# Window attention and two feed-forward layers on one core: means of v from pairs added by GpSimd, unread products in the first microseconds, the first h ahead of the transposes, all keys loaded ahead of v

## The chip, the core and the metric

One core of a Trainium2 chip runs the whole program. It has five engines, each with its own queue of instructions in program order: TensorE (PE in the profile) multiplies matrices into PSUM, VectorE (DVE), ScalarE (ACT) and GpSimd (POOL) work elementwise, and SyncE (SP) here issues every DMA. An engine that waits for a semaphore holds up everything behind it in its own queue. The metric is the device time of one execution in microseconds (us), the median of the runs; less is better.

## What is computed

The output is a chain of three: attention in a window with block summaries, then two feed-forward layers. Cut to what matters:

```python
# q, k, v: 2 batches, 8 heads, 768 positions, 64 wide
k_sum = k.reshape(B, H, nb, 32, D).max(axis=3)     # block maxima of the keys
v_sum = v.reshape(B, H, nb, 32, D).mean(axis=3)    # block means of v
scores_l = scale * q @ k.T, masked to |i - j| < 16
scores_s = scale * q @ k_sum.T + log(32)
a = softmax(concat(scores_l, scores_s))
x = a @ concat(v, v_sum)                           # 1536 tokens, 512 wide

h = x @ w_in                                       # 512 -> 2048
g = max(h, 0) + alpha * min(h, 0)
x = g @ w_out                                      # 2048 -> 512

h = x @ w_in2; g = P(h) / (Q(h) + 1e-6)            # rational function
out = g @ w_out2
```

## The kernel before

The feed-forward products run on operands that are split into a high and a low part, each of which PE multiplies in fp32r: three products (high x high, high x low, low x high) make one. `h_mm` makes h for 128 of the 2048 inner columns in twelve products, `y_mm` adds these 128 inner columns to y in twelve. Weights come as 1 MB transfers (`raw`), and a sequence of steps takes each apart: `top` on ScalarE, `cv` on VectorE ("low"), the high part on ScalarE ("hi": wih, woh), and the two halves of the low part on GpSimd ("mid", "end": wil, wol).

Attention goes by tiles of 64 queries, 24 of them (n). One tile passes through: `qk` (scores s on PE, for four pairs of heads), `mask` and `max` on VectorE, `exp` on ScalarE, `sum`, `guard` and `inv` for the divisor, `norm` (p times 1/d, on GpSimd or VectorE), `turn` (PE transposes p into PSUM, pt), `turned` (ScalarE copies it to pT), `pv` (PE: po), `out` and `outl` (po split into the high and low x, xh on ScalarE and xl on VectorE). PSUM holds one tile each of s, pt and po.

A first loop runs over steps t = -1 to 27. In each step the list of `ORDERS` for the phase of t is gone through, word by word, and each word issues the work of one stage, for n = t plus an offset (qk of t, exp of t - 1, turn of t - 2, pv of t - 3). This fixed order is the order on each engine: nothing is moved at run time. `ENG` says which engine a copy or small step has in each of six phases. "H" and "Y" issue h and y of the first feed-forward layer in the gaps of attention: H from t = 6, Y from t = 9. After the loop the rest of the h and y runs alone, to the end at about 616 us.

The block means of v need all positions of a batch. `att_vload` loads 128 positions of v (`vt`, four buffers), `att_vmean` multiplies them by a matrix `mean` that has 1/32 in the right places, and adds up six such products in one bank of PSUM (`vps`). `VMEAN_AT` gives the step t of each of the twelve. After the sixth, ScalarE copies the means to SBUF, and GpSimd puts them under the values (`vc`) that pv multiplies. `att_kmax` takes the block maxima of the keys (`kmax` from `kt`), which stand beside the keys of each tile in `kc`. `FIRST` lists the first transfers: k0 and k1 are the two halves of the first batch's keys in four transfers each, v tiles, and q tiles. `keep_busy` multiplies the identity with itself into a bank of PSUM that is not read (`idle`).

Of the kernel before, what the change touches and what calls it, by code (L numbers as in the profile page):

```python
# [9 lines left out]
F32 = mybir.dt.float32  # L10
# [21 lines left out]
N_FIRST = 3  # L32
EARLY = 8

VMEAN_AT = (-1, -1, 0, 0, 1, 2, 6, 7, 8, 9, 9, 9)
VLOAD_T = 4
KMAX_AT = (6, 6, 6, 7, 9, 9, 9, 10)
KLOAD_AT = (4, 7)
# [5 lines left out]
     "guard v act in act H gh new"),  # L44
    ("act qk sum hi mid turn act vm k act mask in exp v vmean gh gl max pv ks guard out inv sub low turned "
     "end Y outl kmax H new norm"),
    ("qk vm k exp hi act mask max pv sum out Y turn sub mid inv gl guard in low outl act v vmean act norm H "
     "turned new ks end kmax gh"),
    ("gh qk act pv ks act act exp out end mask hi k sum gl max vmean outl low kmax turn guard mid Y v vm in "
     "sub inv turned new H norm"),  # L50
# [3 lines left out]
     "low guard ks Y end H norm"),  # L54
)

FIRST = 'k0 v0 v1 k1 q0 q2 v2 v3 q1'

SOFTMAX = 'aaaassasaasssabssssssass'

ENG = {"guard": "vapppv", "k": "vpaaaa", "turned": "aaaaaa", "vm": "apppaa", "ks": "ppppav", "norm": "vppppp", "sub": "pppppp",
       "gl": "vvvppp", "gh": "vapaaa", "hi": "vaaaaa", "mid": "pvpppp", "end": "pppppp", "out": "aaaaaa", "al": "vavaaa"}

LEAD = (4, 6, 4, 4, 9, 13, 5, 10)
# [1 line left out]
CLOSE_E = 10  # L66
NKC = 2
VM_WITH = {0: (0, 1), 1: (2, 3)}
BUSY = {(3, 'pv'): 6, (4, 'pv'): 4, (5, 'qk'): 4, (6, 'qk'): 2}


@with_exitstack
def kernel(
# [228 lines left out]

    ident = a1.tile([P, P], F32, name="ident")
    make_identity(nc, ident)
    NQZ, NVC, NVT = 3, 4, 4
    vlate = []
    HALF = S // 2 + 2 * WINDOW
    HSUB = NSUB // 2
    NV = S // P
    bias = []  # L310
    for e in range(3):
        t = a1.tile([P, KEYS], F32, name=f"bias{e}")
# [13 lines left out]
    qz = [b1.tile([P, NPAIR, 2 * QS], F32, name=f"qz{i}") for i in range(NQZ)]  # L326
    kc = [b1.tile([P, NPAIR, KEYS], F32, name=f"kc{i}") for i in range(NKC)]
    vc = [a1.tile([KEYS, DM], F32, name=f"vc{i}") for i in range(NVC)]
    mean = e1.tile([P, KEYS + NB - P // BLOCK], F32, name="mean")
    nc.gpsimd.memset(mean, 0.0)  # L330
    for i in range(P // BLOCK):
        c0 = KEYS - P // BLOCK + i
        nc.gpsimd.memset(mean[i * BLOCK:(i + 1) * BLOCK, c0:c0 + 1], 1.0 / BLOCK)
    kt, kmax, vt, vmean, st = {}, {}, {}, {}, {}

    def att_load(b, half):
# [12 lines left out]
            axis=AX.X, op=ALU.max)  # L349

    def att_vload(b, i):
        vt[b, i] = e1.tile([P, DM], F32, tag="vt", name="vt", bufs=NVT)
        s0 = WINDOW + i * P
        nc.sync.dma_start(out=vt[b, i], in_=vS[b, s0:s0 + P, :])

    def att_vmean(b, i):

        if i == 0:
            vmean[b] = psy.tile([P, 512], F32, tag=f"y{b}", name="vps")
        z0 = (NV - 1 - i) * (P // BLOCK)  # L360
        nc.tensor.matmul(out=vmean[b][0:KEYS, :], lhsT=mean[:, z0:z0 + KEYS], rhs=vt[b, i],  # L361
                         start=(i == 0), stop=(i == NV - 1))
        n = b * NV + i + NVT
        if n < B * NV:
            vlate.append(n)
        if i == NV - 1:
            ps, vmean[b] = vmean[b], (b1 if b else e1).tile([KEYS, DM], F32, tag=f"vmean{b}", name=f"vmean{b}")
            nc.scalar.copy(vmean[b][STRIP:KEYS, :], ps[STRIP:KEYS, :])
# [215 lines left out]
    with tc.manual_schedule():  # L584
        for step in FIRST.split():
            {"k": lambda i: att_load(0, i), "v": lambda i: att_vload(0, i), "q": att_in}[step[0]](int(step[1]))
        for i in range(2 * NPAIR):
            att_kmax(0, i)
        for i, at in enumerate(VMEAN_AT):
            if at == -2:  # L590
                att_vmean(*divmod(i, NV))
        for t in range(-1, LAST + 1):
            now[0] = t
            if t == CLOSE_E:
                att_e.close()
                w_place(1)
            if t == NQ:
                att_qk.close()
                w_place(2)
            if t == 4:  # L600
                nc.sync.dma_start(out=al, in_=alpha)
            if t == 8:
                nc.sync.dma_start(out=na, in_=pa.partition_broadcast(P))
                nc.sync.dma_start(out=ab, in_=pb.partition_broadcast(P))
            if t == 12:
                nc.scalar.mul(na, na, -1.0)
                nc.scalar.activation(out=ab, in_=ab, func=AF.Abs)
            if t in KLOAD_AT:
                att_load(1, KLOAD_AT.index(t))
            act = acts.pop(0) if acts else iter(())  # L610
            g = later.pop(t, None)
            for step in ORDERS[sum(t >= at for at in PHASES)].split():
                if step in attn:
                    f, o = attn[step]
                    for n in {t + o, t + o - (o < -1)}:
                        if 0 <= n < NQ and n - t - o == -(o < -1 and n >= EARLY):
                            f(n)
                    keep_busy(t, step)
                elif step in every:
                    every[step](t)  # L620
                elif step == "act":
                    next(act, None)
                elif step in ("gh", "gl"):
                    if g:
                        (g_split if step == "gh" else g_low)(*g)
                else:
                    w_step(step, 2 if step == "new" else 0)
            if t in WLOAD_AT:
                w_load(*loads.pop(0))
        for act in acts:  # L630
            for _ in act:
                pass
        for t in sorted(later):
            g_split(*later[t])
            g_low(*later[t])
# [104 lines left out]
```

## Time and profile before

| what | value |
|---|---|
| median of 3 runs | 617.39 us (616.64 to 617.71) |
| the profiled execution | 617.73 us |
| its span, first to last instruction | 615.9 us |
| PE busy | 597.7 us (97%), 3224 products |
| VectorE, ScalarE, GpSimd busy | 338.7, 379.9, 358.4 us |
| DMA | 55.09 MB, 89 GB/s on average, over 300 GB/s in most of the first 46 us |
| chain that ended last | PE 76%, VectorE 11%, ScalarE 6%, DMA 3% |

The span begins with the first instruction and is 1.8 us shorter than the time of its execution. A product in fp32 (all of attention) shows in the profile as two rows, one in fp32r as one. The shares are averages over a first stage, in which all engines and the DMA take turns, and a long second one. The granted clock of PE is given as a share of full speed.

### The profile page before, as it was taken

To read this page: it belongs to the slowest core of one execution; us is meant where nothing else is said; L and a number is where in the kernel's file an instruction comes from. 1 tells how busy PE (TensorE), PEld (TensorE's weight loads), DVE (VectorE), ACT (ScalarE), POOL (GpSimd) and SP (SyncE) were. 2 spreads that over 40 slices of the span, in tenths; PEclk is the share of its full clock that TensorE was granted. 3 is DMA by queue.
4 is the path that set the end of the run, shared out by engine and by line. 5 is a ranking of instruction groups with operands and counts; after the bars stand their busy time and mean duration, and the time that the engine had idled before them with its cause. 6 is when DMAs were issued, how large, how long until landed. Compare 5 with 4: busy or idle time off the path is not lost.

```text
span 615.9 us, 8657 instructions
## 1 busy us (share of the span) xinstructions
PE 597.7 (97%) x3224; PEld 498.4 (81%) x3224; DVE 338.7 (55%) x494; ACT 379.9 (62%) x659; POOL 358.4 (58%) x349
## 2 busy tenths in 40 slices
PE   5989999999999999999999999999999999999996
PEld 2767989988888888888888888888888888888884
DVE  4767687753221111145555277776566666566664
ACT  1768898877443333367777467776566666566663
POOL 3467789666612222237777558776466666466662
PEclk9989999999999999999999999999999999999999
DMA  8997566525100000024555101000100000100001
GB/s 299 323 349 248 199 211 220 194 81 206 68 1 1 1 0 1 0 87 187 205 180 185 48 0 69 0 2 1 68 2 1 0 1 1 69 0 2 2 0 68
DMA packets 17129, 55.09 MB, mean 89 GB/s; under 512 B 2368, under 2 KB 4416, under 8 KB 12992
## 3 DMA queue, kind: packets, MB, share of 16 engines
q1 hardware_dynamic: 17088, 54.55, 25.2%
q8 instruction: 25, 0.41, 0.3%
q14 instruction: 16, 0.13, 0.1%
HBM read 51.39 MB, written 3.15 MB: 89 GB/s over the span
## 4 chain that ended last, share of the span: by engine, by line
PE 76%; DVE 11%; ACT 6%; DMA 3%; POOL 2%; issue 1%; SPq 1%; DVEq 0%; ACTq 0%
PE h L197 35%; PE y L260 35%; DVE tp L232 2%; PE s L403 2%; DVE tp L222 2%; DVE h L231 2%; DVE tu L230 2%; DMA kt<-in_kT 2%; ACT h L228 2%; ACT h L229 2%; DVE tp L221 1%; PE vps L361 1%; PE pt L459 1%; PE po L473 1%; DMA qz<-in_qT 1%
## 5 line engine op out<-in xcount | busy, mean ns | idle before, releaser
L197 PE MATMUL h<-xh,wih 128*128 128x512 f32 (+1 forms) x416 | 156.4, 376 | 0.5 <-DVE tp L210 0.5
L197 PE MATMUL h<-xl,wih 128*128 128x512 f32 (+1 forms) x416 | 155.4, 374 | 0.0
L197 PE MATMUL h<-xh,wil 128*128 128x512 f32 (+1 forms) x416 | 155.2, 373 | 0.0
L244 POOL TENSOR_TENSOR gl<-tp,gh 128x512 fp32r<-128x512 f32 (+1 forms) x75 | 95.2, 1270 | 80.1 <-ACT gh L139 78.6
L139 ACT ACTIVATE gh<-tp 128x512 fp32r<-128x512 f32 (+1 forms) x76 | 46.2, 608 | 91.5 <-DVE tp L232 44.6
L197 PEld LDWEIGHTS h<-xh,wih 128*128 128x128 f32 x416 | 78.7, 189 | 15.0 <-DVE tp L210 0.7
L197 PEld LDWEIGHTS h<-xl,wih 128*128 128x128 f32 x416 | 78.6, 189 | 14.0 <-issue 0.5
L197 PEld LDWEIGHTS h<-xh,wil 128*128 128x128 f32 x416 | 78.6, 189 | 13.8
L260 PE MATMUL y<-gh,woh 128*128 128x512 f32 (+1 forms) x224 | 81.9, 366 | 0.0
L260 PE MATMUL y<-gh,wol 128*128 128x512 f32 (+1 forms) x224 | 80.4, 359 | 0.0
L260 PE MATMUL y<-gl,woh 128*128 128x512 f32 (+1 forms) x224 | 80.3, 359 | 0.0
L260 PE MATMUL y<-woh,gh 128*128 128x512 f32 x192 | 74.8, 390 | 1.1 <-ACT gh L139 1.1
L165 DVE SCALAR_TENSOR_TENSOR cv<-raw,top 128x1024 int32<-128x1024 int32 x32 | 58.8, 1838 | 30.4 <-ACT top L163 23.9
L260 PE MATMUL y<-wol,gh 128*128 128x512 f32 x192 | 74.7, 389 | 0.0
L260 PE MATMUL y<-woh,gl 128*128 128x512 f32 x192 | 74.5, 389 | 0.0
L230 DVE SCALAR_TENSOR_TENSOR tu<-tu,h 128x512 f32<-128x512 f32 x48 | 33.0, 687 | 71.0 <-ACT h L229 67.5
L219 POOL TENSOR_SCALAR tu<-tv,ab 128x512 f32<-128x512 f32 x48 | 37.2, 776 | 57.9 <-ACT tv L217 57.9
L220 POOL TENSOR_TENSOR tu<-tu,tv 128x512 f32<-128x512 f32 x48 | 62.3, 1298 | 4.0
L244 POOL TENSOR_TENSOR gl<-tu,gh 128x512 fp32r<-128x512 f32 (+1 forms) x28 | 33.2, 1184 | 49.0 <-ACT gh L139 48.9
L210 DVE SCALAR_TENSOR_TENSOR tp<-h,tp 128x512 f32<-128x512 f32 (+1 forms) x28 | 17.2, 614 | 69.0 <-ACT tp L139 69.0
L228 ACT ACTIVATE h<-tu,lnb 128x512 f32<-128x512 f32 x48 | 33.2, 692 | 35.1 <-DVE tp L222 32.7
L210 DVE SCALAR_TENSOR_TENSOR tu<-h,tu 128x512 f32<-128x512 f32 (+1 forms) x28 | 17.2, 613 | 62.0 <-ACT tu L139 62.0
(83 smaller groups left out, 1066.9 us busy)
## 6 DMA issues: line engine op xcount, KB each, us to landing
raw<-in_w_in SPq DMA_DIRECT2D x16, 1024.0 KB, 4.6
raw<-in_w_out SPq DMA_DIRECT2D x16, 1024.0 KB, 4.6
qz<-in_qT SPq DMA_DIRECT2D x25, 256.0 KB, 5.2
vc<-in_vS SPq DMA_DIRECT2D x24, 192.0 KB, 5.2
kt<-in_kT SPq DMA_DIRECT2D x16, 208.0 KB, 5.0
vt<-in_vS SPq DMA_DIRECT2D x12, 256.0 KB, 5.1
out<-stage SPq DMA_DIRECT2D x12, 256.0 KB, 2.1
al<-in_alpha SPq DMA_DIRECT2D x1, 8.0 KB, 5.5
```

The costliest lines, as they stand in the source:

```text
L139: e.activation(out=out, in_=in_, func=AF.Copy, scale=1.0 if scale is None else scale)
L165: nc.vector.scalar_tensor_tensor(out=w.bitcast(I32), in0=rest, scalar=13, in1=top, op0=ALU.logical_shift_right, op1=ALU.bitwise_or)
L197: nc.tensor.matmul(out=ps, lhsT=a, rhs=b, start=(c == 0 and m == 0), stop=(c == NC - 1 and m == 2))
L210: nc.vector.scalar_tensor_tensor(out=t, in0=ps, scalar=0.0, in1=t, op0=ALU.max, op1=ALU.subtract)
L219: nc.gpsimd.tensor_scalar(out=q, in0=v, scalar1=ab[:, 1:2], scalar2=ab[:, 0:1], op0=ALU.mult, op1=ALU.add)
L220: nc.gpsimd.tensor_tensor(out=q, in0=q, in1=v, op=ALU.mult)
L222: nc.vector.scalar_tensor_tensor(out=p, in0=p, scalar=na[:, 1:2], in1=ps, op0=ALU.add, op1=ALU.mult)
L228: nc.scalar.activation(out=A, in_=q, func=AF.Ln, scale=2.0 ** -LN_SHIFT, bias=lnb)
L229: nc.scalar.activation(out=A, in_=A, func=AF.Exp, scale=-1.0, bias=exb)
L230: nc.vector.scalar_tensor_tensor(out=q, in0=q, scalar=one, in1=A, op0=ALU.add, op1=ALU.mult)
L244: (eng("gl") if (u, f) != steps[-1] else nc.vector).tensor_tensor(out=gl, in0=t, in1=gh.bitcast(F32), op=ALU.subtract)
L260: nc.tensor.matmul(out=yps[c][:, c0:c0 + n] if layer == 0 else yps[c], lhsT=a, rhs=b, start=(f == 0 and c0 == 0 and m == 0), stop=(f == NF ...
```

## The change

Four things. A tile of v now holds 256 positions, two consecutive ones in each partition; GpSimd adds the two, and PE multiplies the sum, so that there are three products for a batch instead of six, and two buffers instead of four. `mean` is built with 16 partitions to a block. `FIRST` loads both halves of the keys, then q0 and q1, and only then v. Eighteen products of the identity stand first on PE, and more of them at t = 6 (three behind qk, three behind pv). In the list of t = 5 and 6, pv and out come earlier, H comes ahead of turn and vmean, outl ahead of the "low" step, and guard moves from GpSimd to VectorE, ahead of inv.

```diff
-VMEAN_AT = (-1, -1, 0, 0, 1, 2, 6, 7, 8, 9, 9, 9)
+VMEAN_AT = (0, 1, 2, 6, 7, 9)
...
-    ("qk vm k exp hi act mask max pv sum out Y turn sub mid inv gl guard in low outl act v vmean act norm H "
-     "turned new ks end kmax gh"),
+    ("qk pv vm k exp out hi act mask max sum guard inv outl H Y turn sub mid norm gl in low act v vmean act "
+     "turned new ks end kmax gh"),
...
-FIRST = 'k0 v0 v1 k1 q0 q2 v2 v3 q1'
+FIRST = 'k0 k1 q0 q1 v0 q2 v1'
...
-ENG = {"guard": "vapppv", "k": "vpaaaa", "turned": "aaaaaa", "vm": "apppaa", "ks": "ppppav", "norm": "vppppp", "sub": "pppppp",
+ENG = {"guard": "vavppv", "k": "vpaaaa", "turned": "aaaaaa", "vm": "apppaa", "ks": "ppppav", "norm": "vppppp", "sub": "pppppp",
...
-BUSY = {(3, 'pv'): 6, (4, 'pv'): 4, (5, 'qk'): 4, (6, 'qk'): 2}
+BUSY = {(-2, ''): 18, (3, 'pv'): 6, (4, 'pv'): 4, (5, 'qk'): 4, (6, 'qk'): 3, (6, 'pv'): 3}
...
-    NQZ, NVC, NVT = 3, 4, 4
+    NQZ, NVC, NVT = 3, 4, 2
...
-    NV = S // P
+    NV = S // (2 * P)
...
-        vt[b, i] = e1.tile([P, DM], F32, tag="vt", name="vt", bufs=NVT)
-        s0 = WINDOW + i * P
-        nc.sync.dma_start(out=vt[b, i], in_=vS[b, s0:s0 + P, :])
+        vt[b, i] = e1.tile([P, 2, DM], F32, tag="vt", name="vt", bufs=NVT)
+        s0 = WINDOW + i * 2 * P
+        nc.sync.dma_start(out=vt[b, i], in_=vS[b, s0:s0 + 2 * P, :].rearrange("(p a) c -> p a c", a=2))
...
-        z0 = (NV - 1 - i) * (P // BLOCK)
-        nc.tensor.matmul(out=vmean[b][0:KEYS, :], lhsT=mean[:, z0:z0 + KEYS], rhs=vt[b, i],
+        z0 = (NV - 1 - i) * VB
+        v = vt[b, i]
+        nc.gpsimd.tensor_tensor(out=v[:, 0, :], in0=v[:, 0, :], in1=v[:, 1, :], op=ALU.add)
+        nc.tensor.matmul(out=vmean[b][0:KEYS, :], lhsT=mean[:, z0:z0 + KEYS], rhs=v[:, 0, :],
                          start=(i == 0), stop=(i == NV - 1))
...
+        keep_busy(-2, "")
         for i in range(2 * NPAIR):
             att_kmax(0, i)
```

At t = 5 and 6 the order on PE stands as follows, first before the change, from the scores of t = 5 to the first product of h.

```order
L403 MATMUL s<-kc_182,qz_180 128x120 x4
L494 MATMUL idle<-ident 128x128 x4
L473 MATMUL po<-pT,vc_185 64x64 x8
L459 MATMUL pt<-ident,p 120x128 x4
L403 MATMUL s<-kc_181,qz_178 128x120 x4
L494 MATMUL idle<-ident 128x128 x2
L473 MATMUL po<-pT,vc_186 64x64 x8
L459 MATMUL pt<-ident,p 120x128 x4
L361 MATMUL vps<-vt,mean 120x512
L197 MATMUL h<-xh,wih_432 128x256
```

After the change, on PE from the scores of t = 6 to those of t = 7, of the twelve products of h the first and the last:

```order
L410 MATMUL s<-kc_181,qz_178 128x120 x4
L501 MATMUL idle<-ident 128x128 x3
L480 MATMUL po<-pT,vc_186 64x64 x8
L501 MATMUL idle<-ident 128x128 x3
L197 MATMUL h<-xh,wih_450 128x256
...
L197 MATMUL h<-xh,wil_451 128x256
L466 MATMUL pt<-ident,p 120x128 x4
L368 MATMUL vps<-vt,mean 120x512
L410 MATMUL s<-kc_182,qz_179 128x120 x4
```

The first h has moved ahead of the transposes and the product of v, and behind a second set of unread products.

On GpSimd at t = 8 and 9, before the change, from the first gl to the second guard:

```order
L244 TENSOR_TENSOR gl<-tu,gh 128x256
L445 TENSOR_SCALAR d<-d 128x4
L175 TENSOR_TENSOR wol_637<-cv,woh_636 128x512
L453 TENSOR_TENSOR p<-p,d 128x480
L175 TENSOR_TENSOR wol_637<-cv,woh_636 128x512
L244 TENSOR_TENSOR gl<-tp,gh 128x256
L445 TENSOR_SCALAR d<-d 128x4
```

And after the change, the same stretch on GpSimd:

```order
L244 TENSOR_TENSOR gl<-tu,gh 128x256
L452 TENSOR_SCALAR d<-d 128x4
L175 TENSOR_TENSOR wol_650<-cv,woh_649 128x512
L460 TENSOR_TENSOR p<-p,d 128x480
L175 TENSOR_TENSOR wol_650<-cv,woh_649 128x512
L244 TENSOR_TENSOR gl<-tp,gh 128x256
L367 TENSOR_TENSOR vt<-vt 128x512
L452 TENSOR_SCALAR d<-d 128x4
```

The add of the last pair of v stands behind norm (p times d), half of wol and gl.

## Rows read from the trace of the kernel before

**Rows 1.** Table by stages: stretch, length, busy us (instructions) of PE, PEld, DVE, ACT, POOL, clock, DMA, GB/s

```profile
54.80:100.00 45.20, 43.63 (x447) 41.69 (x446) 32.73 (x61) 40.61 (x94) 37.02 (x39) 1.00 0.65 221
100.00:600.00 500.00, 500.00 (x2423) 417.02 (x2422) 262.75 (x356) 301.14 (x468) 289.04 (x247) 1.00 0.15 54
```

**Rows 2.** Timeline of GpSimd, the identity: start, duration, instruction

```profile
1.18 0.30 POOL masks.py:199 TENSOR_SCALAR_AFFINE_SELECT ident<-ident 128x128 f32<-128x128 f32 x1
```

**Rows 3.** Timeline of PE, 0 to 17 us: start, duration, instruction, idle before

```profile
6.88 3.74 PE L361 MATMUL vps<-vt,mean 128*120 128x512 f32 x4 [6.88 <-POOL bias L323]
11.07 2.06 PE L403 MATMUL s<-kc,qz 128*128 128x120 f32 x8 [0.44 <-POOL kc L141]
12.92 3.28 PE L361 MATMUL vps<-vt,mean 128*120 128x512 f32 x4
16.04 1.05 PE L403 MATMUL s<-kc,qz 128*128 128x120 f32 x8
```

**Rows 4.** Timelines of VectorE and ScalarE, the last four maxima and the first means

```profile
8.38 2.25 DVE L346 TENSOR_REDUCE kmax<-kt 128x12 f32<-128x384 f32 x4 [1.67 <-DMA kt<-in_kT]
...
21.12 0.58 ACT L368 COPY vmean<-vps 24x512 f32<-24x512 f32 x1 [0.26 <-PE vps L361]
```

**Rows 5.** Timelines of PE and ScalarE, t = 6 and 7

```profile
33.87 0.69 PE L473 MATMUL po<-pT,vc 120*64 120x64 f32 x16 [1.28 <-ACT kc L139]
35.98 0.93 PE L459 MATMUL pt<-ident,p 128*120 128x128 f32 x4 [1.42 <-POOL p L453]
...
37.63 1.20 PE L197 MATMUL h<-xh,wih 128*128 128x256 f32 x1
...
40.38 1.05 PE L403 MATMUL s<-kc,qz 128*128 128x120 f32 x8
...
37.01 0.60 ACT L139 ACTIVATE pT<-pt 120x512 f32<-120x512 f32 x1 [1.75 <-PE pt L459]
```

**Rows 6.** Table by stages, three single microseconds

```profile
9.00:10.00 1.00, 1.00 (x2) 0.04 (x1) 0.99 (x2) 0.00 (x0) 0.00 (x0) 1.00 1.04 393
35.00:36.00 1.00, 0.02 (x1) 0.02 (x1) 0.97 (x4) 0.26 (x1) 1.00 (x2) 1.00 1.08 449
37.00:38.00 1.00, 1.00 (x3) 0.36 (x2) 0.48 (x2) 0.60 (x1) 1.00 (x2) 0.50 1.02 416
```

**Rows 7.** Chain that ended last, a later h: start, duration, what

```profile
59.91 1.50 PE h L197 x12
```

**Rows 8.** Timeline of PE, t = 9

```profile
51.17 0.69 PE L473 MATMUL po<-pT,vc 120*64 120x64 f32 x16
51.79 2.83 PE L361 MATMUL vps<-vt,mean 128*120 128x512 f32 x6
54.46 0.60 PE L459 MATMUL pt<-ident,p 128*120 128x128 f32 x4
54.82 0.36 PE L260 MATMUL y<-gh,woh 128*128 128x256 f32 x1
```

**Rows 9.** Timeline of GpSimd, t = 8 and 9

```profile
52.38 0.99 POOL L453 TENSOR_TENSOR p<-p,d 128x480 f32<-128x480 f32 x1 [1.25 <-DVE d L449]
53.33 1.28 POOL L175 TENSOR_TENSOR wol<-cv,woh 128x512 fp32r<-128x512 f32 x1
54.58 0.73 POOL L244 TENSOR_TENSOR gl<-tp,gh 128x256 fp32r<-128x256 f32 x1
```

**Rows 10.** DMA issues at 6.76 and 17.12 us: count, size, us to landing

```profile
vt<-in_vS SPq DMA_DIRECT2D x1, 256.0 KB, 5.3
...
qz<-in_qT SPq DMA_DIRECT2D x1, 256.0 KB, 2.5
```

**Rows 11.** Timelines of GpSimd and VectorE, t = 5

```profile
32.45 2.12 POOL L175 TENSOR_TENSOR wil<-cv,wih 128x512 fp32r<-128x512 f32 x1 [0.57 <-ACT wih L139]
...
34.94 0.99 POOL L453 TENSOR_TENSOR p<-p,d 128x480 f32<-128x480 f32 x1
...
32.24 1.19 DVE L165 SCALAR_TENSOR_TENSOR cv<-raw,top 128x1024 int32<-128x1024 int32 x1
```

More of the change, by code (lines that the diff above doesn't have):

```diff
@@ L328 @@
     vc = [a1.tile([KEYS, DM], F32, name=f"vc{i}") for i in range(NVC)]
-    mean = e1.tile([P, KEYS + NB - P // BLOCK], F32, name="mean")
+    VB = 2 * P // BLOCK
+    mean = e1.tile([P, KEYS + NB - VB], F32, name="mean")
     nc.gpsimd.memset(mean, 0.0)
-    for i in range(P // BLOCK):
-        c0 = KEYS - P // BLOCK + i
-        nc.gpsimd.memset(mean[i * BLOCK:(i + 1) * BLOCK, c0:c0 + 1], 1.0 / BLOCK)
+    blocks = mean[:, KEYS - VB:KEYS]
+    nc.gpsimd.memset(blocks, 1.0 / BLOCK)
+    rows = BLOCK // 2
+    nc.gpsimd.affine_select(out=blocks, in_=blocks, compare_op=ALU.is_ge, fill=0.0,
+                            base=0, pattern=[[-rows, VB]], channel_multiplier=1)
+    nc.gpsimd.affine_select(out=blocks, in_=blocks, compare_op=ALU.is_ge, fill=0.0,
+                            base=rows - 1, pattern=[[rows, VB]], channel_multiplier=-1)
     kt, kmax, vt, vmean, st = {}, {}, {}, {}, {}
@@ L617 @@
                             f(n)
-                    keep_busy(t, step)
                 elif step in every:
@@ L627 @@
                     w_step(step, 2 if step == "new" else 0)
+                keep_busy(t, step)
             if t in WLOAD_AT:
```

## The prediction

> **What bounds the kernel now.** I read a table by stages first: from 100 to 600 us TensorE (PE) is busy 500.00 of 500.00 us, and from 54.8 to 100 us 43.63 of 45.20 [rows 1]. So from the first product of y at 54.82 us on, PE runs almost without a gap, and nothing in the diff changes its work after that product. The end therefore moves by as much as that first y moves, and only what happens in the first 55 us has to be worked out. There I read the timeline of each engine. "t" is the step of the first loop; y first runs at t = 9.
>
> Four places matter. At the start PE waits until 6.88 us for constants, multiplies two tiles of v at 3.74 us for the pair, starts the first scores at 11.07, two more tiles of v at 12.92, and the second scores only at 16.04 [rows 3]. That stretch runs at half speed: the first scores take 2.06 us, the second, of the same shape, 1.05 [rows 3]. The keys hold it up too: VectorE takes the last four block maxima from 8.38 us on, 2.25 us for the four [rows 4], each behind its own transfer. The first batch's means leave at 21.12 us on ScalarE [rows 4].
>
> At t = 6 PE waits 1.28 us ahead of po and 1.42 us ahead of the transposes (pt), and the first h follows at 37.63 us [rows 5]. In 35 to 36 us PE is busy 0.02 us, and in 37 to 38 the granted clock is 0.50 [rows 6], that is 1.2 of 2.4 GHz: the twelve products of the first h run from 37.63 until the scores at 40.38, 2.75 us [rows 5]; a later h takes 1.50 [rows 7].
>
> At t = 9 PE ends po and starts three products of v at 51.79 us, pt at 54.46 and y at 54.82 [rows 8]. GpSimd meanwhile does norm at 52.38, half of wol at 53.33, gl at 54.58 and is free at about 55.3 [rows 9].
>
> **The change part by part.** *Keys ahead of v.* Two transfers of v, 512 KB, no longer stand ahead of the second half of the keys. At 393 GB/s [rows 6] they are 1.3 us. The last maximum starts at about 8.38 + 3 x 0.56 = 10.07 now, so at 8.7, and the first scores at some 9.7 instead of 11.07.
>
> *Unread products at the start.* 18 of 128x128. The trace has the same instruction only at full clock inside t = 3 and later; taken as half a cold 120-column score product of 2.06 / 4 = 0.5 us [rows 3], all 18 take 9 us at the low clock and half of that at the high one. They start when the identity is there, at 1.5 us [rows 2], so they end between 6 and 10.6 us; they lie in time that PE waits anyway, and the first scores then run in about 1 us instead of 2.06. If they ended last they would cost up to 0.9 us there.
>
> *Pairs.* A tile of v is now 512 KB in two rows per partition, six instead of twelve, with two buffers. PE loses six products of 128x512 of about 0.9 us, but of these only the ones at t = 8 and 9 (three) stand near the path. Each of the six now waits for an add on GpSimd. No row shows that add; the nearest are norm, 128x480 in 0.99 us, and wol, 128x512 in 1.28 us [rows 9]. I take 1.05, between 0.99 and 1.28.
>
> The start, then: the first pair stands behind eight keys and two q. The second q and the v ahead of it are about what was in front of the third v tile before, and that landed 5.3 us after its issue at 6.76, at 12.1 [rows 10]; with 0.25 MB less ahead of it, 11.4. The add ends at 12.5, the product at 13.4. Only then is the buffer free, so the transfer of the third pair is issued at 13.4. A 256 KB transfer on idle queues landed after 2.5 us, one in a full queue after 5.3 [rows 10]; 512 KB with little ahead: 3.6 (2.5 to 5.3). So 17.0, the add 18.05, the product 19.0, and ScalarE copies the means at 19.1 to 19.5 instead of 21.12 [rows 4]. pv, and with it all of t = 3 to 5, depends on that copy. **Gain 1.8 us** (0 if the transfer takes 5.3 and PE has fallen to the low clock again; 3 if the first pair lands at 10.6 and the third in 2.8).
>
> *First h ahead of pt, pv and outl earlier, guard on VectorE.* In the clock of the trace of before: outl of t = 5 moves ahead of cv, so po starts 1 us earlier than 33.87. The h waits for the low half of x (outl of t = 6), about 36.4, and is done at 37.9 if the clock holds. That is 2.5 us before 40.38. But then pt, and behind pt the product of a pair whose add stands on GpSimd behind sub, half of wil (2.12 us, 32.45 to 34.57), norm, the other half, half of the next wil and the next norm [rows 11]: 34.6 + 1.0 + 1.25 + 1.25 + 1.0 + 1.05 = 40.1. The product ends at 41.0, so the next scores start there and not at 40.38. Also ScalarE now gets pt later (38.4 against 37.01 for its copy), and only then takes the next weights apart. So h is earlier and nothing behind it is: **+0.2 us** (-0.8 to +0.8). Of the two guards that leave GpSimd nothing is left in that sum. The six extra unread products here lie in a wait.
>
> *Pair of t = 9.* This is the largest term. Before, the three products at 51.79 needed only data that had landed, and filled PE while GpSimd finished norm [rows 8, 9], which pt needs. After, one product waits for an add that stands behind norm, wol and gl: GpSimd is free for it at 55.3, it ends at 56.35, the product at 57.25, pt at 57.65, and y starts at 57.65 instead of 54.82. Everything that sets this (the norm, po) comes from the same h two products earlier, so a shift of the start moves both and does not close the gap. **Cost 2.8 us** (2.2 to 3.4). Queued behind that product on PE are pt, y and the scores; behind ScalarE's copy of the second means, pT and the next top.
>
> *Clock.* PE is then empty from 51.8 to 56.35 us, 4.5 us. The gap that cost the clock before was 1.28 + 1.42 us with 0.7 us of work between [rows 5, 6]. A longer one should cost as much: 2.75 - 1.50 = 1.25 us [rows 5, 7]. I take **1.0** (0 to 1.25), since it may partly fall into the wait.
>
> Sum: -1.8 + 0.2 + 2.8 + 1.0 = +2.2 us. The profiled execution took 617.73 us, so 619.9; the median of the runs, 617.39, is 0.34 us under it, so **619.6 us**.
>
> **A rule weighed.** VectorE's cv runs from 32.24 us, and the wil that GpSimd starts at 32.45 takes 2.12 us where wol, of the same shape, takes 1.28 [rows 9, 11]; it ends 1.1 us after cv does. The Trainium skill, SBUF — State Buffer, in its rules on the shared port pair, says that VectorE and GpSimd hold that pair exclusively for a whole instruction, and that the one that issues second is blocked until the first is done, when VectorE has two inputs in SBUF and GpSimd reads SBUF. The trace agrees with it here. By it an add is as long as its neighbour on VectorE allows.
>
> **The rivals.** *Faster.* The add at t = 9 is not late: GpSimd gets there with norm done early, for instance because VectorE reaches the reciprocal of t = 8 sooner without guard traffic. Then y starts as soon as norm allows, 53.33 + 0.1 + 0.4 = 53.85, 1.0 us before 54.82, and the start's gain stays: 617.4 - 1.8 - 1.0 + 0.2 = 614.8 us, 613.6 with a start of -3. It decides if norm at t = 8 ends 2.8 us earlier against po than in rows 8 and 9. For it: PE loses 2.7 us of products there. Against: norm waits for VectorE, and no edit is made in the steps 7 to 9 but the adds. Chance 0.22.
>
> *No change.* The stall is there, but the start gains 3 us and the clock holds: 617.4 - 3 + 2.8 + 0.2 = 617.4. Chance 0.23.
>
> *The lock.* Adds and cv meet at t = 6 or 9 and one waits for the other, 1.2 us by the wil above [rows 11]: 619.6 + 1.2 = 620.8, up to 622. Chance 0.10; the page's rule is the one named above.
>
> *The products at the start do nothing.* PE falls back before the scores and the start gains 0.5: 620.9. This lies in the forecast's range.
>
> **How the numbers follow.** Forecast, 618.6 to 621.6: 0.45, its own range by the bounds of the terms; faster 0.22; no change 0.23; the lock 0.10. A measurement of this kernel tells about 0.2%, 1.2 us, from nothing, so under 616.2 is faster and over 618.6 slower: by the cases 0.22, 0.23 and 0.55. The range reaches down to 614.9, over most of the faster case, and up to 621.6; about 2 in 10 is left out.
>
> **What the profile will show.** Right: the first scores near 9.7 us and at full speed; the copy of the first means near 19.3; first h done well before the following scores; PE empty some 4.5 us ahead of the pair's product at t = 9, released by GpSimd's add, with the granted clock at 0.50 behind it; y first at about 56 us. Wrong: that product runs right behind po, or y starts before 54.8 us; or GpSimd's adds take far over 1.3 us; or PE has new gaps after 60 us, so that y's start no longer sets the end.

## The result and the profile after

The changed kernel takes 625.15 us (median of 4 runs, 624.99 to 626.23), the kernel before 617.01 us beside it on the same chip (4 runs, 615.65 to 617.71): 8.1 us more, a ratio of 1.0138 [1.0126, 1.0150]. The forecast was 619.6 us, at most 621.6. The sign was right and the size was not.

The table by stages of the changed kernel answers to [rows 1] and [rows 6]; the columns are those of rows 1.

```profile
14.00:16.00 2.00, 2.00 (x7) 1.29 (x6) 0.00 (x0) 1.57 (x8) 1.01 (x1) 0.50 0.33 126
...
38.00:40.00 2.00, 1.44 (x11) 1.44 (x12) 1.87 (x5) 0.00 (x0) 2.00 (x2) 0.98 0.98 382
40.00:42.00 2.00, 1.66 (x7) 1.12 (x6) 0.00 (x0) 0.84 (x2) 2.00 (x3) 0.50 1.04 418
...
56.00:58.00 2.00, 0.00 (x0) 0.00 (x0) 2.00 (x5) 1.39 (x3) 2.00 (x3) 0.75 0.88 332
58.00:60.00 2.00, 0.84 (x1) 0.47 (x2) 0.36 (x2) 0.00 (x0) 1.83 (x3) 0.50 0.92 343
...
54.80:100.00 45.20, 40.01 (x383) 37.38 (x384) 29.05 (x58) 35.95 (x90) 33.50 (x36) 0.92 0.57 188
100.00:600.00 500.00, 499.30 (x2456) 417.40 (x2455) 264.30 (x360) 303.55 (x474) 290.55 (x249) 1.00 0.16 58
```

From 100 us on PE is as full as before: 499.30 of 500 us. What was lost lies ahead of it, at three places where the granted clock also falls to 0.50: about 14 us, 40 us (behind the first h, which still runs at 0.98) and 58 us. The timeline of PE shows them (start, duration, instruction, idle time before it and what ended it); it answers to [rows 3, 5, 8].

```profile
1.59 6.27 PE L501 MATMUL idle<-ident 128*128 128x128 f32 x36 [1.59 <-POOL ident masks.py:199]
10.21 1.15 PE L410 MATMUL s<-kc,qz 128*128 128x120 f32 x8 [2.34 <-POOL bias L323]
13.19 2.06 PE L368 MATMUL vps<-vt,mean 128*120 128x512 f32 x2 [1.83 <-POOL vt L367]
...
20.78 1.12 PE L368 MATMUL vps<-vt,mean 128*120 128x512 f32 x2 [0.38 <-POOL vt L367]
...
31.80 1.15 PE L410 MATMUL s<-kc,qz 128*128 128x120 f32 x8
...
35.30 0.37 PE L197 MATMUL h<-xh,wih 128*128 128x256 f32 x1
38.56 0.39 PE L197 MATMUL h<-xl,wih 128*128 128x256 f32 x1 [2.89 <-DVE xl L494]
...
40.01 1.06 PE L466 MATMUL pt<-ident,p 128*120 128x128 f32 x4
41.41 2.06 PE L368 MATMUL vps<-vt,mean 128*120 128x512 f32 x2 [0.34 <-POOL vt L367]
43.26 1.09 PE L410 MATMUL s<-kc,qz 128*128 128x120 f32 x8
...
53.77 0.69 PE L480 MATMUL po<-pT,vc 120*64 120x64 f32 x16
59.16 2.06 PE L368 MATMUL vps<-vt,mean 128*120 128x512 f32 x2 [4.70 <-POOL vt L367]
61.01 1.06 PE L466 MATMUL pt<-ident,p 128*120 128x128 f32 x4
61.73 0.56 PE L260 MATMUL y<-gh,woh 128*128 128x256 f32 x1
...
64.17 1.05 PE L410 MATMUL s<-kc,qz 128*128 128x120 f32 x8
```

Three more rows of the kernel before are needed as marks, two of PE's timeline and one of VectorE's:

```profile
30.99 1.15 PE L403 MATMUL s<-kc,qz 128*128 128x120 f32 x8
...
56.63 1.04 PE L403 MATMUL s<-kc,qz 128*128 128x120 f32 x8
...
35.71 0.39 DVE L487 TENSOR_TENSOR xl<-po,xh 128x256 fp32r<-128x256 f32 x1
```

The first y starts at 61.73 us, 6.9 after that of before, and the scores behind its twelve products at 64.17, 7.5 after 56.63. The span ends 7.4 us later. Between those scores and the end nothing is lost, so the shift of 7.54 us is the sum to be explained. It adds up from the same marks in both traces: scores of t = 6 31.80 for 30.99, **+0.8**; from these to the scores of t = 7 11.46 for 9.39, **+2.1**; from there to po of t = 9 10.51 for 10.79, **-0.3**; from po to the scores of t = 10 10.40 for 5.46, **+4.9**.

On GpSimd the adds and what stands around them (the first two rows lie at the start, the next four at t = 5 and 6, the last four at t = 8 and 9, and answer to [rows 9, 11]):

```profile
11.87 1.26 POOL L367 TENSOR_TENSOR vt<-vt 128x512 f32<-128x512 f32 x1 [1.53 <-DMA vt<-in_vS]
...
19.45 1.28 POOL L367 TENSOR_TENSOR vt<-vt 128x512 f32<-128x512 f32 x1 [4.44 <-DMA vt<-in_vS]
...
33.53 1.27 POOL L175 TENSOR_TENSOR wil<-cv,wih 128x512 fp32r<-128x512 f32 x1 [0.84 <-ACT wih L139]
34.76 1.97 POOL L460 TENSOR_TENSOR p<-p,d 128x480 f32<-128x480 f32 x1
36.70 2.50 POOL L175 TENSOR_TENSOR wil<-cv,wih 128x512 fp32r<-128x512 f32 x2
...
40.10 1.26 POOL L367 TENSOR_TENSOR vt<-vt 128x512 f32<-128x512 f32 x1
...
54.99 0.99 POOL L460 TENSOR_TENSOR p<-p,d 128x480 f32<-128x480 f32 x1 [1.25 <-DMA na<-in_pa]
55.93 1.27 POOL L175 TENSOR_TENSOR wol<-cv,woh 128x512 fp32r<-128x512 f32 x1
57.17 0.72 POOL L244 TENSOR_TENSOR gl<-tp,gh 128x256 fp32r<-128x256 f32 x1
57.85 1.26 POOL L367 TENSOR_TENSOR vt<-vt 128x512 f32<-128x512 f32 x1
```

An add takes 1.26 to 1.28 us wherever it stands. At t = 9 it waits for nothing of its own: it is queued behind norm, wol and gl and starts as soon as gl is done, at 57.85. PE, which ended po at 54.46, starts the product at 59.16. (The name behind an arrow is inferred and can mislead: norm at 54.99 follows VectorE's reciprocal, which ends at 54.91, as it did before, and not the small transfer `na`, and e1 and e3 name that reciprocal at this place; the first scores at 10.21 follow the copies to `kc`, which end at 10.15, and not the memset of `bias`.)

The timelines of VectorE, ScalarE and SyncE's issues, the rows that answer to [rows 4, 10, 11] and the low half of x that the first h waits for:

```profile
7.05 2.72 DVE L351 TENSOR_REDUCE kmax<-kt 128x12 f32<-128x384 f32 x5 [0.44 <-DMA kt<-in_kT]
...
33.57 2.32 DVE L165 SCALAR_TENSOR_TENSOR cv<-raw,top 128x1024 int32<-128x1024 int32 x1
...
38.11 0.39 DVE L494 TENSOR_TENSOR xl<-po,xh 128x256 fp32r<-128x256 f32 x1
...
21.94 0.58 ACT L375 COPY vmean<-vps 24x512 f32<-24x512 f32 x1 [0.90 <-PE vps L368]
...
15.28 0.33 SPq L359 DMA_DIRECT2D vt<-in_vS  x1
```

cv takes 2.32 us here and 1.19 before [rows 11]. The third pair's transfer is issued at 15.28, when the half-speed product of the first pair (13.19 to 15.04) has given the buffer back.

### The profile page after: what moved, and what is told of

It is laid out like the page before. It is cut to its first block, busy times and chain, and to the rows that moved or that the text cites. A ratio compares the mean times of both kernels' runs of the same rounds, so it can differ in the third digit from the quotient of the medians.

```text
span 623.3 us, 8721 instructions
## 1 busy us (share of the span) xinstructions
PE 600.7 (96%) x3256; PEld 504.6 (81%) x3256; DVE 340.6 (55%) x496; ACT 379.9 (61%) x659; POOL 364.8 (59%) x352
## 2 busy tenths in 40 slices
DMA packets 16265, 55.09 MB, mean 88 GB/s; under 512 B 2272, under 2 KB 4320, under 8 KB 12128
## 4 chain that ended last, share of the span: by engine, by line
PE 74%; DVE 10%; ACT 6%; DMA 5%; POOL 3%; issue 1%; SPq 1%; DVEq 0%; ACTq 0%; POOLq 0%
PE h L197 35%; PE y L260 35%; DVE tp L232 2%; DVE tp L222 2%; DVE h L231 2%; DVE tu L230 2%; ACT h L228 2%; DMA kt<-in_kT 2%; ACT h L229 2%; DVE tp L221 1%; DMA vc<-in_vS 1%; PE po L480 1%; PE s L410 1%; PE vps L368 1%; PE pt L466 1%
```

## The experiments

In the expectations, A says that the waits for the adds cost the time, above all at t = 9; B that the fallen clock does; C that the adds make GpSimd slow; D that the order and the adds lose what the start wins; E that v itself comes late; F that a gain at the start is lost at t = 7, where ScalarE waits for the first transfer of w_out; G that VectorE and GpSimd hold each other up at cv; H is the contrary of F or D where it is named. All differences below are to the kernel before on the same chip (616.65 to 617.51 us), by medians; those between two changed kernels are differences of these. None of these kernels leaves out a part of the computation; where products are added at the start or in a wait, nothing reads them.

This table has the marks of the profiled executions (us): ScalarE's copy of the first means, the scores of t = 6 and of t = 7, the first y.

| kernel | copy | s, t = 6 | s, t = 7 | first y | time against before |
|---|---|---|---|---|---|
| before | 21.12 | 30.99 | 40.38 | 54.82 | |
| after | 21.94 | 31.80 | 43.26 | 61.73 | +8.1 |
| e1 last pair at t = 8 | 21.41 | 31.69 | 43.52 | 58.79 | +4.3 |
| e2 no adds | 19.30 | 30.33 | 43.51 | 56.77 | +2.3 |
| e3 products in the wait of t = 9 | 21.77 | 31.78 | 43.60 | 61.20 | +5.8 |
| e4 30 products at the start | 21.05 | 31.27 | 42.54 | 61.26 | +7.8 |
| e5 keys first | 20.98 | 32.23 | 40.01 | 56.29 | +2.3 |
| e6 order alone | 19.42 | 29.56 | 41.39 | 55.94 | +2.3 |
| e7 18 products alone | 19.53 | 30.08 | 39.49 | 55.09 | +1.5 |
| e8 pairs and adds, old order | 22.75 | 32.88 | 46.37 | 65.17 | +10.7 |
| e13 no adds, old order | 19.85 | 30.91 | 39.55 | 55.90 | +1.5 |

**e1, the last pair a step earlier.**

```diff
-VMEAN_AT = (0, 1, 2, 6, 7, 9)
+VMEAN_AT = (0, 1, 2, 6, 7, 8)
```

> The changed kernel with the last pair of v added and multiplied at t = 8 in place of t = 9. Theory A (the wait of PE for the add at t = 9 is the largest loss): PE waits for the add at t = 8 instead, 1.5 to 2.5 us ahead of the transposes there, and the 4.7 us ahead of the last product at t = 9 are gone with the half clock behind it; the first y moves from 61.7 to about 57 us and the time from 625.2 to 620 to 621.5. Theory B (the loss is the clock of PE, which falls three times) expects the fall at 56 us to go, about 2 us: 623. Theory C (adds slow GpSimd down wherever they stand) expects no change, 625.

621.81 us, ratio 1.0069 [1.0052, 1.0086]. The wait went along, as A had it: 2.79 us ahead of the product at t = 8 (A: 1.5 to 2.5, and 621.5 us at most) instead of 4.70 at t = 9.

```profile
52.43 1.12 PE L368 MATMUL vps<-vt,mean 128*120 128x512 f32 x2 [2.79 <-POOL vt L367]
```

Half of the loss hangs on where this one add stands.

**e2, no adds at all.**

```diff
-        nc.gpsimd.tensor_tensor(out=v[:, 0, :], in0=v[:, 0, :], in1=v[:, 1, :], op=ALU.add)
-        nc.tensor.matmul(out=vmean[b][0:KEYS, :], lhsT=mean[:, z0:z0 + KEYS], rhs=v[:, 0, :],
-                         start=(i == 0), stop=(i == NV - 1))
+        for a in range(2):
+            nc.tensor.matmul(out=vmean[b][0:KEYS, :], lhsT=mean[:, z0:z0 + KEYS], rhs=v[:, a, :],
+                             start=(i == 0 and a == 0), stop=(i == NV - 1 and a == 1))
```

> The changed kernel without the adds: PE multiplies both rows of a pair, so there are twelve products again, and each waits for its transfer alone. Everything else is as changed. Theory A: 4.5 us from t = 9, some 1.3 us of the start, since the third transfer waits for the first product, and 0.3 at t = 6: about 619. Theory B: the gaps that lower the clock shrink, the same 619, but with the granted clock at full speed throughout. Theory C: all of the loss, 617 or less.

619.80 us, 1.0038 [1.0023, 1.0053]: PE does six products more and the kernel is 5.8 us faster for it (8.1 less 2.3; 5.4 by the two medians themselves). The wait at t = 9 is gone. What stays lies at t = 6, as PE's timeline of this kernel shows:

```profile
37.09 0.58 PE L197 MATMUL h<-xl,wih 128*128 128x256 f32 x1 [2.90 <-DVE xl L494]
...
40.45 3.23 PE L368 MATMUL vps<-vt,mean 128*120 128x512 f32 x4
```

The same wait inside h, and behind it the two products of a pair (four rows) in 3.23 us; at t = 7 they take 1.98. The copy of the first means came 2.6 us earlier than in the changed kernel, but the scores of t = 7 did not come earlier (43.51 for 43.26): what the kernel wins by losing the adds, it wins between there and y.

**e3 and e4, the clock.** Unread products in the wait of t = 9, and more of them at the start.

```diff
-BUSY = {(-2, ''): 18, (3, 'pv'): 6, (4, 'pv'): 4, (5, 'qk'): 4, (6, 'qk'): 3, (6, 'pv'): 3}
+BUSY = {(-2, ''): 18, (3, 'pv'): 6, (4, 'pv'): 4, (5, 'qk'): 4, (6, 'qk'): 3, (6, 'pv'): 3, (9, 'pv'): 16}  # e3
+BUSY = {(-2, ''): 30, (3, 'pv'): 6, (4, 'pv'): 4, (5, 'qk'): 4, (6, 'qk'): 3, (6, 'pv'): 3}  # e4
```

> The changed kernel with 16 more unread products behind po of t = 9, which fill the wait of PE there (16 x 0.27 = 4.3 us). Theory A: the wait for the add stays, and only the half clock behind it goes, 0.95 us of the product of v, 0.3 of the transposes and 0.95 of the first y: about 623. Theory B: the clock is most of it, 621 or less. Theory C: no change.

> The changed kernel with 30 in place of 18 unread products at the start, which should end near 11.1 us. Theory A: the first scores start 0.9 us later, but the clock stays up until 19 us, the first product of v ends about 1 us earlier, and so does the third transfer: 624 to 625. Theory B: the lost clock of 12 to 19 us comes back, about 3 us: 622. Theory C: no change.

e3: 623.29 us, 1.0093 [1.0078, 1.0108]. PE's timeline:

```profile
55.10 3.84 PE L501 MATMUL idle<-ident 128*128 128x128 f32 x32
59.89 1.12 PE L368 MATMUL vps<-vt,mean 128*120 128x512 f32 x2 [0.95 <-POOL vt L367]
```

The add comes no earlier (4.08 us after the start of po in both), but the product behind it takes 1.12 us and not 2.06, and y follows at full speed. The fallen clock at t = 9 is worth about 2 us: 2.4 by 8.1 less 5.8, 1.9 by the two medians themselves, 2.0 from po to the next scores in the two profiles. So A was right, at 623, and B, at 621 or less, was not. e4: 625.32 us, 1.0126 [1.0110, 1.0141], the same as the changed kernel. Behind the unread products its start runs at full speed (the first product of v takes 1.12 us), and its copy comes 0.9 us earlier, but the gap at t = 9 is 4.71 us and the time is the same.

**e5 to e8, the parts alone, on the kernel before.**

```diff
-FIRST = 'k0 v0 v1 k1 q0 q2 v2 v3 q1'
+FIRST = 'k0 k1 q0 q1 v0 v1 q2 v2 v3'                        # e5, first products of v at t = 0, 0, 1, 1, 2, 2
+    ("qk pv vm k exp out hi act mask max sum guard inv outl H Y turn sub mid norm gl in low act v vmean act "   # e6, with the guards and the unread products of t = 6
+BUSY = {(-2, ''): 18, (3, 'pv'): 6, (4, 'pv'): 4, (5, 'qk'): 4, (6, 'qk'): 2}   # e7
```

e8 is the changed kernel with the order, guards and unread products of before and v between the two halves of the keys.

> The kernel before with all keys, then q0 and q1, loaded ahead of v, twelve single tiles of v as before (their products at t = 0, 0, 1, 1, 2, 2 in the first batch). Theory D (the order at t = 5 and 6 and the adds lose, the edits at the start gain): the first scores near 9.7 us, the copy of the first means 0.5 to 1.5 us earlier than 21.1, the time 616 to 617.5. Theory E (v loaded late is what loses at the start): the copy later than 21.1 us, 618 or more.

> The kernel before with only the new order of t = 5 and 6 (h ahead of the transposes, pv and outl earlier, guard on VectorE) and its unread products there; no pairs, no adds, the old start. Theory D: PE waits some 2.9 us inside the first h for the low half of x, its clock falls, and the scores of t = 7 start 2 to 4 us after 40.4: 619.5 to 621.5. Rival (the order is harmless, the adds behind it lose): the scores of t = 7 at 40 us, 617.5 or less.

> The kernel before with only the 18 unread products at the start. Theory D: they end near 7.9 us, the first products of v start 1 us later but run at full speed, as do the next two, and the second scores start 1 us or more before 16.0: 616 to 617. Rival (the clock falls again behind them): no change, 617.5.

> The kernel before with only the pairs: six tiles of 256 positions, added by GpSimd, at the steps of the changed kernel, v loaded between the halves of the keys as before, the old order, no products at the start. Theory A and D: the gap of 4.7 us at t = 9 with its half clock is here too, 4 to 5 us, and the start is 0 to 1.5 us later: 621.5 to 623.5. Rival (the pairs lose only together with the new order): 619 or less.

Each part alone makes the kernel slower; of e7 neither theory had expected that. e5: 618.97, 1.0040 [1.0025, 1.0055]; the first scores are there at 9.77 us, but w_in and w_out come later, and ScalarE waits 1.67 and 2.28 us for them. So E had the time of e5 and not the reason: its copy is not later. e6: 618.90, 1.0038 [1.0023, 1.0052]; the wait inside h is 2.90 us and the clock is 0.50 behind it, as D had it, though the scores of t = 7 come 1.0 us later and not 2 to 4. e7: 618.19, 1.0031 [1.0019, 1.0044]; ScalarE's timeline:

```profile
39.65 1.37 ACT L163 ACTIVATE top<-raw 128x1024 f16<-128x1024 bf16 x1 [3.01 <-DMA raw<-in_w_out]
```

e8: 627.35, 1.0177 [1.0162, 1.0192], the slowest, 4 us above the 621.5 to 623.5 that A and D expected. With the old order the product of a pair at t = 6 stands ahead of h and takes the wait for the add with it:

```profile
41.95 2.06 PE L368 MATMUL vps<-vt,mean 128*120 128x512 f32 x2 [3.42 <-POOL vt L367]
...
62.60 2.06 PE L368 MATMUL vps<-vt,mean 128*120 128x512 f32 x2 [4.70 <-POOL vt L367]
```

So the new order loses 2.3 us on the kernel before (e6) and seems to save about that much where there are adds (10.7 less 8.1, though e8 differs in its start too). The parts don't add up.

**e9 to e12, where the start's gain goes.** v of the second batch behind w_out; e10 the same with the 18 products, e12 also without the early second transfer of q. e11 is e6 with cv ahead of the low half of x.

```diff
-VLOAD_T = 4
-VMEAN_AT = (-1, -1, 0, 0, 1, 2, 6, 7, 8, 9, 9, 9)
+VLOAD_T = 6                                        # e9
+VMEAN_AT = (-1, -1, 0, 0, 1, 2, 8, 8, 8, 9, 9, 9)
-... max sum guard inv outl H Y turn sub mid norm gl in low act v vmean ...
+... max sum guard inv low outl H Y turn sub mid norm gl in act v vmean ...   # e11
```

> The kernel before with the second batch's v loaded from t = 6 on, behind the first two transfers of w_out, its products at t = 8 and 9 (three each). Theory F (what is gained ahead of t = 6 is lost at t = 7, where ScalarE waits for the first transfer of w_out, which stands behind 1 MB of v): that transfer lands 1 to 2.5 us earlier than 38.6 us, the first y up to 2 us earlier: 615 to 616.5. Rival (the chain of h, top and cv sets that stretch, the transfer is in time): no change, 617.

> The same with the 18 unread products at the start as well. Theory F: the start's 1 to 1.6 us, which were lost behind the transfer, now reach the first y: 614 to 616. Rival: the products cost something in themselves, 618 as in the run with them alone.

> The kernel before with the new order of t = 5 and 6, and in it the weights' step on VectorE (cv) ahead of outl again. Theory G (cv waits because GpSimd's wil starts first and holds the port): cv of t = 5 takes 1.2 us again and wil 2.1, the low half of x is ready about 1 us earlier, and PE waits 1.9 us in the first h, not 2.9: 0 to 1.5 us faster than the order alone, 617.5 to 619. Rival (cv takes 2.3 us for another reason): it stays at 2.3, no change.

> The kernel of the second run of this group without the early load of q2, which is loaded again at t = -1 in all kernels so far: 256 KB less. Theory F: everything behind it on the queues is 0.6 us earlier, and so is the time: 0.3 to 0.6 us under the second run. Rival: no change.

e9: 618.92 us (616.17 to 622.51, 12 runs), 1.0039 [1.0021, 1.0057]. In its profile w_out is no longer waited for, but two products of v at t = 9 wait 1.99 us for their transfers. e10: 619.36, 1.0045 [1.0027, 1.0064], 2.62 us of the same wait. e12: 619.47, 1.0034 [1.0016, 1.0051]. F had forecast 614 to 616.5 us for the first two; they are slower than before, and e12 gained nothing on e10. F was half right: the wait at t = 7 can be removed, and another takes its place.

e11: 618.36, 1.0017 [1.0008, 1.0026], 1.2 us over the kernel before where e6 is 2.3 (the intervals touch). The timelines of VectorE and GpSimd, first of e6, then of e11:

```profile
31.33 2.31 DVE L165 SCALAR_TENSOR_TENSOR cv<-raw,top 128x1024 int32<-128x1024 int32 x1
...
35.49 0.25 DVE L445 TENSOR_SCALAR d<-d 128x4 f32<-128x4 f32 x1
...
31.29 1.28 POOL L175 TENSOR_TENSOR wil<-cv,wih 128x512 fp32r<-128x512 f32 x1 [0.85 <-ACT wih L139]
```

```profile
30.53 1.20 DVE L165 SCALAR_TENSOR_TENSOR cv<-raw,top 128x1024 int32<-128x1024 int32 x1
...
33.91 1.15 DVE L445 TENSOR_SCALAR d<-d 128x4 f32<-128x4 f32 x1
...
30.80 2.06 POOL L175 TENSOR_TENSOR wil<-cv,wih 128x512 fp32r<-128x512 f32 x1 [0.84 <-ACT wih L139]
...
33.78 2.48 POOL L175 TENSOR_TENSOR wil<-cv,wih 128x512 fp32r<-128x512 f32 x2
```

cv is short again, as G had it, and now wil is long. PE's wait inside h is 1.80 us instead of 2.90, but mostly because h starts 0.9 us later after the scores of t = 6 (4.40 for 3.49). The low half of x comes only 0.2 us earlier after them (6.12 for 6.31): the guard, moved to VectorE, takes 1.15 us instead of 0.25, and another wil had started 0.13 us ahead of it. The lock moved from one instruction to another.

**e13 and e14, what is left without adds.** e13 is e2 with the order, guards and unread products of t = 5 and 6 as before; e14 is e2 with cv ahead of the low half of x, as in e11.

> The changed kernel without the adds (both rows of a pair go through the products, two for each pair), and with the order, the guards and the unread products of t = 5 and 6 as they were before; the 18 products at the start, the keys ahead of v and the pairs of 512 KB stay. D (the adds cost 5.35 us, and what is left over the kernel before, 2.8 us, is the order at t = 5 and 6, where h waits inside for the low half of x): no wait inside h, h behind the product of v, 617.2 to 618.2 us, and the scores of t = 7 no later than 41 us. H (what is left comes from the first transfers and from the transfers of 512 KB, not from the order): 619 us or more, with PE waiting for a transfer of v, of raw weights or of q in the first 45 us.

> The changed kernel without the adds, with the order of the change, but the low half of the weights (cv) ahead of the low half of x (outl) on VectorE. G (cv and GpSimd's wil hold each other up; with cv first, cv takes about 1.2 us instead of 2.3 and wil 2.1 instead of 1.3, and the low half of x comes about 1.1 us earlier): the wait inside h is 1.8 us instead of 2.9, 619.3 us, 0.5 under the same kernel with outl first. D without G (the length of cv does not matter, since h ahead of the transposes delays them anyway): 619.8 us, the same.

e13: 618.86, 1.0022 [1.0009, 1.0035]; e14: 619.47, 1.0036 [1.0023, 1.0050]. In e13 the wait inside h is gone and the scores of t = 7 come at 39.55, 4.0 us before those of e2, as D had it; yet the time is only 0.8 us better (1.5 for 2.3, intervals that overlap) and lies between D's 618.2 at most and H's 619 at least. ScalarE now waits for w_out, a transfer, as H had it:

```profile
40.68 1.36 ACT L163 ACTIVATE top<-raw 128x1024 f16<-128x1024 bf16 x1 [3.43 <-DMA raw<-in_w_out]
```

G's half microsecond in e14 can't be told from nothing.

**e15 to e17, v between the two places.** The kernel before with v of the second batch released at t = 5; e15 and e16 with the 18 products.

```diff
-VLOAD_T = 4
+VLOAD_T = 5                                         # e15, e16, e17
-VMEAN_AT = (-1, -1, 0, 0, 1, 2, 6, 7, 8, 9, 9, 9)
+VMEAN_AT = (-1, -1, 0, 0, 1, 2, 7, 8, 8, 9, 9, 9)   # e16, e17
```

> The kernel before with the 18 unread products at the start, and the transfers of v for the second batch released at t = 5 instead of t = 4. F (the gain at the start is lost at t = 7, where ScalarE waits about 3 us for the first w_out transfer behind v's transfers; with v released at t = 6 that wait was gone, but v came 2 to 2.6 us late at t = 9): in between, the wait at t = 7 shrinks to 0 to 1.5 us and v at t = 9 is late by 0 to 1 us, 616.5 to 617.5 us, the same as before or a little faster. H (any release moves the wait from one place to the other): 618 to 619 us.

> The kernel before with the 18 unread products at the start, the transfers of v for the second batch released at t = 5, and the products of these tiles at t = 7, 8, 8, 9, 9, 9 instead of 6, 7, 8, 9, 9, 9, so that none is needed at t = 6, where the release at t = 5 made PE wait 4.70 us for v. F (the start's gain of about 1.6 us is real and is lost to w_out at t = 7, or to v where v comes later): no wait over 0.5 us for a transfer at t = 7, at most 1 us for v at t = 9, y at 53.5 to 54.5 us, 615.8 to 617 us, faster than before by 0.4 to 1.5. H (the transfers are full until about 45 us, and any order of them makes some engine wait): y at 55 us or later, 618 us or more.

> The same without the unread products at the start: the kernel before with v of the second batch released at t = 5 and its products at t = 7, 8, 8, 9, 9, 9. F: the difference to the run with the products at the start is what the start is worth once no transfer eats it, 1 to 1.6 us, so 617 to 618 us. H: the same time as with them, 618 us or more in both.

e15: 624.06, 1.0103 [1.0090, 1.0116], a miss for both theories. Its first product of v is still at t = 6, ahead of h, and waits for the later transfer:

```profile
41.73 2.06 PE L361 MATMUL vps<-vt,mean 128*120 128x512 f32 x2 [4.70 <-DMA vt<-in_vS]
```

It is the changed kernel's gap made by a transfer, of the same 4.70 us, with the same half-speed product behind it, and the kernel is 6.7 us slower than before. e16: 617.37, 1.0008 [0.9996, 1.0020], the same as before; no wait for a transfer on PE is over 0.2 us and y starts at 54.10. That is where F had y, but not F's time (faster by 0.4 to 1.5), and it is not H's 618 or more either. e17: 618.27, 1.0021 [1.0008, 1.0033]. That the start's products bring the 0.9 us between e16 and e17 is not shown: the intervals overlap, the copy of the first means is in e16's profile the later one (20.79 for 19.55), and e17's has a wait of 1.83 us for a transfer of v at t = 7 that e16's has not. No version tried was faster than the kernel before.

## Why the prediction was wrong

The sum was -1.8 + 0.2 + 2.8 + 1.0 = +2.2 us; the traces give +0.8, +1.8 (2.1 - 0.3) and +4.9, together 7.5. The 5.3 us between them are 2.6 of the start, 1.6 of t = 5 and 6, and 1.1 of t = 9.

**The step that failed first: the start, "Gain 1.8 us".** The chain was the right one and every link came late: the first pair's add started at 11.87 (11.4 forecast), the third pair's transfer was issued at 15.28 (13.4), its add started at 19.45 (17.0), the copy came at 21.94 (19.1 to 19.5). The clock was the largest link. I took the 18 products to carry full speed into the first product of v; but PE waits 2.34 us for the keys and 1.83 for the add, the clock falls to 0.50, and the product takes 2.06 us. e4, in which it takes 1.12, has its copy 0.9 us earlier. I had named that case in the bound "0", and it was worse than the bound.

Behind it is a second error that the experiments showed: one execution was taken as the kernel's start. Five profiled executions with the first transfers and first products of before have their copy at 21.12 (before), 19.42 (e6), 20.37 (e9), 19.20 (e11) and 19.55 (e17). The trace that I read was the latest of them. Four with the 18 products (e7, e10, e15, e16) have 18.83 to 21.42 (e12, without the early q, 20.98), three with the transfers of the change and no adds (e2, e13, e14) 19.30 to 21.09, and the three with the adds (after, e1, e3) 21.41 to 21.94. Means of 19.9, 20.1, 20.1 and 21.7: products and transfers gain nothing there that can be told from this scatter, and the adds seem to lose some 1.6 us, which three profiles don't settle (e4, with adds and 30 products, has 21.05). The rival "the products at the start do nothing" had the clock nearly right, which fell behind the first scores and not ahead of them, but gave the start a gain of 0.5 us all the same. That the loss against the median of before (8.1) is larger than that between the two profiles (7.3) fits this.

Nor does a shift of the start go through to y, as the sum assumed: in e7, e9 and e10 it ended at a wait for w_out or v. In the changed kernel it did go through: +0.8 at the copy and +0.8 at the scores of t = 6.

**t = 5 and 6, "+0.2 us".** The working itself makes more of it: the next scores at 41.0 and not at 40.38 are +0.6. And the unread products there are four more, not six (six for two). I wrote that h "is done at 37.9 if the clock holds". The clock held: the granted clock is 0.98 in 38 to 40 us, and the eleven products behind the wait run from 38.56 to 40.01, 1.45 us. But h was done at 40.01, since the low half of x came at 38.11, 6.31 us after the scores where before it was 4.72 (35.71 less 30.99). PE waited 2.89 us inside h, and behind h the clock fell to 0.50: the product of the pair took 1.85 us until the next scores (41.41 to 43.26) instead of 0.9. That is 0.95 us for which I had booked nothing at this place. Another 0.5 is the add, which ended at 41.36; my chain of GpSimd has 40.1, with the start's 0.8 40.9. Its wil was short again, but norm behind it took 1.97 us. In e2, e3 and e6 the same wait is there and the clock is 0.50 from 38 us on, within h, so where in this stretch it falls differs.

Why the low half of x came late: of the 1.59 us, cv's 2.32 for 1.19 makes 1.13, and the two guards that moved to VectorE (0.17 and 0.24) make 0.41. Why cv got longer is in the rows: wil starts at 33.53, 0.04 us ahead of cv, and cv ends 1.1 us after wil; before, cv started 0.21 us ahead and wil was the one that took 2.12 [rows 11]. The Trainium skill, SBUF — State Buffer, in "SBUF: two separate sides", says that whichever of the two starts first holds the pair for its whole instruction; the runs here show both sides of it (cv and wil in before and after, e6 and e11). I had weighed this rule for one side only, and not asked which of the two the new order puts first. e11 and e14 say what that was worth: cv short again brought 1.0 us in one and 0.2 in the other, neither clear of the scatter; in both the guard was caught next and took 1.15 us.

**t = 9, "Cost 2.8 us" and the clock "1.0".** The mechanism was right: the gap is 4.70 us, 4.5 forecast, released by the add behind norm, wol and gl. Mis-sized were the add (1.26 us for 1.05, 0.2) and the clock. The product took 1.85 us until pt instead of 0.9, pt 0.72 instead of 0.36, and the twelve products of y 2.44 instead of 1.81: 1.9 us together, which e3 confirms with 1.9 to 2.4. I took the price from one h [rows 5, 7]; here the product of v, pt and most of y's twelve products ran at the low clock.

**The rivals.** "No change" needed a start 3 us earlier and a clock that holds, and neither came. "Faster" fell: norm at t = 8 ends at 55.98, 1.5 us after po ends, and the add stands behind two more. "The lock" struck, but not the adds, which take 1.26 to 1.28 us everywhere. What was to show the forecast right did so for the gap, its releaser, the clock behind it and an h done well before the next scores; the first scores ran at full speed, 0.5 us late (10.21); the copy (19.3 forecast) and the first y (56) were wrong. One slip left the time alone: 2.06 / 4 = 0.5 us is a whole cold score product and not half of one, and the 18 products took 6.27 us in all, within the 4.5 to 9 that followed.

Left open: 2.3 us of the loss remain without the adds (e2). The order alone costs as much (e6), but with the old order 1.5 stay (e13, whose profile has 3.43 us of a wait for w_out), and the difference between the two is not clear of the scatter; so these 2.3 us have no single cause that a run shows. And the runs of e9, e10, e12, e13 and e17 scatter over 3.4 to 6.3 us, those of before beside them over 2.2 to 3.4. One profile of each can't say why.

## What to carry to other kernels

Work taken from a full engine and put on one that is free on average still has a place in that engine's queue: ask what stands ahead of it at each place, for here six adds of 1.26 us that save six products cost 5.4 to 5.8 us. Price a gap on TensorE with the slow work behind it, and compare the start of a kernel over several executions before booking a gain from one. Then follow the gain to the next transfer that everything waits for.

## What the runs showed of the hardware

VectorE and GpSimd hold each other up in both directions, and 0.04 to 0.3 us of order decide which: cv 1.19 and wil 2.12, or cv 2.32 and wil 1.27. Even a guard of 128x4 took 1.15 us right behind the start of a wil (e11, e14), and 0.25 elsewhere (e6).

The granted clock in the profile does not show the slow first microseconds: two products of 128x512 (four rows) took 3.74 us at 6.88 us in before, where the column reads 1.00, and 1.95 us in e7 behind the 18 products. In three of five executions with these products (e12, e15, e16) the next two products still took 3.3 to 3.6 us, behind a wait of 1.8 to 2.1 us ahead of the scores between them, and there the column does read 0.50 to 0.70; e7 waited 1.84 us and kept its speed.
